# Storing eight blocks of the probability matrix p in six pieces each, without the quarter that is never read back

## The chip, the cores and the metric

The kernel runs on one core of one Trainium2 chip. The metric is the device time of one execution in microseconds (us): the median of 3 runs is 1787.07 us before the change, with runs from 1784.61 to 1787.16. One profiled execution, which took 1786.83 us, gives the trace that is read below.

## What is computed

x is a 2048 x 512 matrix in fp32. Its rows are normalised (xn), and two branches are combined:

```
s   = attention(xn @ wq, k_cache[last 512], v_cache[last 512]) @ wo      32 heads of 128
z   = gelu(x @ w_in);  z1, z2 = first half, layernorm(second half)
g   = silu(((w_sp @ z2 + b_sp) * z1) @ w_out)
out = x + s * g
```

For each head, `scores = q k^T / sqrt(128)`, `p = softmax(scores)` over 512 keys, and `o = p v`. The change lies in the attention, in the way in which p is turned from rows of queries to columns of queries.

## The kernel before

Every fp32 product is made of three matmuls on pairs (high part, low part), written `hi, lo`. The attention works on 128 blocks (`NBLK`): a block b is one head and 512 queries, and has 4 steps of 128 queries, so the loop over t has 512 steps (`NSTEP`) and some lead and tail. In one step TensorE (PE) makes the scores of step t (`score`, L65 to L67 on `qT`), 2 or 3 products of the query projection of a later group (`q_products`, L457), the product of p and v of an earlier block (`pv`, L522 to L524) and the output projection of a still earlier one (`outp`, L65 to L67 on `oT`).

p is made with queries on the partitions, and `pv` needs keys there. The 128 x 512 array of a step is turned in two moves. First VectorE (DVE) transposes 32 x 32 blocks (`turn(t)`, L495) into `pL[b]`, a tile of 128 partitions x 4 x 512. What then stands in partition group i (32 partitions) and part a has to go to partition group a and part i. That is done through DRAM: after the fourth step of a block one DMA stores the whole tile, 128 rows of 8 KB, into `pD[b]` (name p_dram, L499), and two steps later `turned(b)` loads it back in six pieces (L507), in which groups and parts have changed places. The quarter with a = i stays where it is and isn't loaded. From the loaded tile ScalarE casts `pT_h` (`shares`, L514), GpSimd makes `pT_l` (L59), and PE multiplies.

All DMAs named here are issued by SyncE (SP), one after the other in program order, so an issue that waits holds back all that follow it. In each block SP issues the store, loads of weights (`raw`, L105, and in every fourth block two of `wq`, L418), and the six loads of `turned`.

The 64 blocks 0 to 63 work on the first 1024 queries, 64 to 127 on the rest. Near the end of the first half the projection has to change to the other half of x: 28 parts of 256 KB (7 operands `ORDER[k]` with 4 parts n each) are fetched from DRAM by `fetch_part` (L273, names x<-x_dram) at steps 228 + (35 + 34k + 8n)/10, that is in steps 231 to 254, one part per step or a little faster; the matmuls at L457 read them from step 244 on. These steps are those of blocks 57 to 63. The blocks 56 to 63 are the ones that the change touches. Part 28 (k = 6, n = 3) comes in step 254, after the six loads of block 62, and is first read in step 259.

```
for k in range(7):
    for n in range(4):
        ends.setdefault(16 * (NG // 2 - 1) - LEAD + (35 + 34 * k + 8 * n) // 10, []).append((fetch_part, 1, ORDER[k], n))
```

Of the kernel before, what the change touches and what calls it, by code (L numbers as in the profile page):

```python
# [28 lines left out]
NBLK = H * NQ  # L29
# [7 lines left out]
Q = 32  # L37
# [3 lines left out]
def mixer_kernel(ctx: ExitStack, tc: tile.TileContext, x, wh, w_in, w_sp, b_sp, w_out, out):  # L41
# [8 lines left out]
    nc = tc.nc  # L50
# [324 lines left out]
    qps, qT, pps, pD, pL, pT, oT, prob, sums = {}, {}, {}, {}, {}, {}, {}, {}, {}  # L375
# [112 lines left out]
    def turn(t):  # L488

        b, j = divmod(t, 4)
        if j == 0:
            pL[b] = ap.tile([P, 4, 512], F32, name="pL", bufs=4)
        nc.vector.transpose(pL[b][:, :, j * P:j * P + P].rearrange("p a (c q) -> p a c q", q=Q),  # L495
                            prob.pop(t).rearrange("p (a c q) -> p a c q", a=4, q=Q))
        if j == 3:
            pD[b] = dram.tile([4, Q, 4, 512], F32, name="p_dram", bufs=3)
            nc.sync.dma_start(pD[b].rearrange("i r a f -> (i r) (a f)"), pL[b].rearrange("p a f -> p (a f)"))  # L499
            nc.vector.reciprocal(sums[b], sums[b])  # L500

    def turned(b):
# [203 lines left out]
    for t in range(T0, T1):  # L706
# [6 lines left out]
        i = t + XL  # L713
# [33 lines left out]
        if 0 <= t - 1 < NSTEP:  # L747
            turn(t - 1)
# [183 lines left out]
    for r in range(RP):  # L932
        f = WHEN[r, "P6"]
# [88 lines left out]
    for r in range(RP):  # L1022
# [3 lines left out]
        f = WHEN[r, "P6"]  # L1026
# [146 lines left out]
```

## Time and profile before

| | |
|---|---|
| median of 3 runs | 1787.07 us |
| profiled execution | 1786.83 us, its span 1785.0 us |
| PE busy | 1767.4 us, 99% of the span |
| DVE, ACT, POOL busy | 1484.7, 1185.8, 1256.3 us |
| DMA | 402.12 MB, 74.3% of the 16 DMA engines' span on SP's queue |
| p stores (L499) | 128 of 1024 KB, median 4.7 us from issue to landing |
| p loads (L507) | 256 each of 192, 128 and 64 KB, median 4.1, 4.0 and 3.9 us |

The profile's busy times are sums over the whole span. Where an engine had to wait, the trace names what released it. For DMAs it has the time of the issue on SP (SPq) and the time from issue to landing; the share of the DMA engines' time can come out a little over 1 in a short stretch, since packets are counted with their whole duration.

### The profile page before, as it was taken

The numbers are of one execution on the slowest core, as the hardware profiler recorded it, in microseconds if no ns is written. First come the engines' busy times: TensorE is split into PE (matmuls) and PEld (weight loads), VectorE is DVE, ScalarE is ACT, GpSimd is POOL, SyncE is SP. The second block draws the span as 40 slices with busy tenths as digits, with TensorE's granted clock in tenths as the row PEclk, the third lists the DMA queues.
The fourth block names the chain that finished last, engine by engine and source line by source line (L and its number), as shares of the span: only waits on it lengthen the run. The fifth ranks groups of instructions, "written<-read, shape, count | busy, mean of one in ns | idle before, by whom it ended". The sixth has DMA issues, their size and how long they took to land.

```text
span 1785.0 us, 28580 instructions
## 1 busy us (share of the span) xinstructions
PE 1767.4 (99%) x8463; PEld 1513.0 (85%) x8463; DVE 1484.7 (83%) x2451; ACT 1185.8 (66%) x2637; POOL 1256.3 (70%) x1195
## 2 busy tenths in 40 slices
PE   9999999999999999899999999999999999999999
PEld 8788888888888888688888888888888999999997
DVE  6789989899999988788888888888889546887775
ACT  5777777777777776577777777777777546543333
POOL 2788898898888988678888888888888425000033
PEclk9999999999999999999999999999999999999999
DMA  5688887988888989787777787777788652655486
GB/s 202 201 234 246 259 258 224 263 245 240 261 242 247 263 234 291 244 261 228 226 223 224 223 229 217 230 216 231 222 227 256 212 184 87 200 185 171 146 246 210
DMA packets 181180, 402.12 MB, mean 225 GB/s; under 512 B 24096, under 2 KB 61216, under 8 KB 161824
## 3 DMA queue, kind: packets, MB, share of 16 engines
q1 hardware_dynamic: 176416, 394.66, 74.3%
q10 hardware_dynamic: 4608, 5.64, 0.9%
q8 instruction: 66, 1.08, 0.3%
q14 instruction: 90, 0.74, 0.2%
HBM read 233.74 MB, written 166.46 MB: 224 GB/s over the span
## 4 chain that ended last, share of the span: by engine, by line
PE 89%; DVE 4%; DMA 3%; ACT 2%; POOL 1%; issue 1%; SPq 0%; ACTq 0%; DVEq 0%; POOLq 0%
PE ps_a L457 15%; PE ps L67 12%; PE ps L65 12%; PE ps L66 12%; PE ps L881 11%; PE ps_a L524 6%; PE ps_a L522 6%; PE ps_a L523 6%; PE ps_a L65 2%; PE ps_a L66 2%; PE ps_a L67 2%; DMA p_dram<-pL 1%; DMA x<-x_dram 1%; PE ps_f L66 1%; PE ps_f L65 1%; PE ps_f L67 1%
## 5 line engine op out<-in xcount | busy, mean ns | idle before, releaser
L59 POOL TENSOR_TENSOR pT_l<-pL,pT_h 128x512 fp32r<-128x512 f32 x507 | 656.6, 1298 | 189.3 <-ACT pT_h L514 180.4
L486 ACT ACTIVATE prob<-ps,nm 128x512 f32<-128x512 f32 x512 | 354.0, 691 | 337.6 <-DVE nm L484 329.7
L546 DVE SCALAR_TENSOR_TENSOR sacc<-ps,sums,sacc 128x512 f32<-128x512 f32 x496 | 369.9, 746 | 128.5 <-PE ps L67 123.1
L457 PE MATMUL ps_a<-x,x 128*128 128x512 f32 x1302 | 376.7, 390 | 5.7 <-DMA x<-x_dram 5.7
L495 DVE STREAM_TRANSPOSE pL<-prob 128x512 f32<-128x512 f32 x512 | 358.9, 701 | 2.8 <-ACT prob L486 2.8
L484 DVE TENSOR_REDUCE nm<-ps 128x1 f32<-128x512 f32 x512 | 340.4, 665 | 4.9 <-PE ps L67 4.9
L514 ACT CAST pT_h<-pL 128x512 fp32r<-128x512 f32 x512 | 318.5, 622 | 21.8 <-DMA pL<-p_dram 8.5
L457 PEld LDWEIGHTS ps_a<-x,x 128*128 128x128 f32 x1302 | 244.4, 188 | 57.6 <-DMA x<-x_dram 4.7
L59 POOL TENSOR_TENSOR wl<-raw,wh 128x512 fp32r<-128x512 f32 x186 | 241.3, 1297 | 11.3 <-ACT wh L144 11.3
L881 PE MATMUL ps<-b,x 128*128 128x344 f32 x1344 | 212.9, 320 | 3.1 <-POOL b L59 1.3
L881 PEld LDWEIGHTS ps<-b,x 128*128 128x128 f32 x1344 | 212.0, 188 | 3.9 <-POOL b L59 1.5
L524 PE MATMUL ps_a<-pT_l,wh 128*128 128x512 f32 x512 | 200.4, 391 | 1.7 <-POOL pT_l L59 1.5
L65 PE MATMUL ps<-wh,qT_h 128*128 128x512 f32 x512 | 200.0, 391 | 0.8 <-DVE sacc L546 0.8
L522 PE MATMUL ps_a<-pT_h,wh 128*128 128x512 f32 x512 | 200.2, 391 | 0.0
L67 PE MATMUL ps<-wh,qT_l 128*128 128x512 f32 x512 | 199.9, 390 | 0.3
L65 PE MATMUL ps<-wh,oT_h 128*128 128x512 f32 x512 | 199.8, 390 | 0.0
L523 PE MATMUL ps_a<-pT_h,wl 128*128 128x512 f32 x512 | 199.5, 390 | 0.0
L67 PE MATMUL ps<-wh,oT_l 128*128 128x512 f32 x512 | 199.5, 390 | 0.0
L66 PE MATMUL ps<-wl,oT_h 128*128 128x512 f32 x512 | 199.4, 390 | 0.0
L66 PE MATMUL ps<-wl,qT_h 128*128 128x512 f32 x512 | 199.3, 389 | 0.0
L59 POOL TENSOR_TENSOR b<-b 128x688 fp32r<-128x688 f32 (+1 forms) x10 | 18.2, 1820 | 216.6 <-ACT b L1049 188.0
L59 POOL TENSOR_TENSOR x<-wq,x 128x256 fp32r<-128x256 f32 x186 | 138.0, 742 | 1.4 <-ACT x L439 1.4
(206 smaller groups left out, 2998.9 us busy)
## 6 DMA issues: line engine op xcount, KB each, us to landing
p_dram<-pL SPq DMA_DIRECT2D x128, 1024.0 KB, 4.7
pL<-p_dram SPq DMA_DIRECT2D x256, 192.0 KB, 4.1
raw<-wh SPq DMA_DIRECT2D x188, 256.0 KB, 6.2
pL<-p_dram SPq DMA_DIRECT2D x256, 128.0 KB, 4.0
x<-w_sp SPq DMA_DIRECT2D x24, 1024.0 KB, 5.2
pL<-p_dram SPq DMA_DIRECT2D x256, 64.0 KB, 3.9
wq<-wh SPq DMA_DIRECT2D x62, 256.0 KB, 5.8
x_dram<-rawx SPq DMA_DIRECT2D x32, 256.0 KB, 6.1
```

What stands on the lines that cost most here:

```text
L59: engine.tensor_tensor(lo, whole, hi.bitcast(F32), op=OP.subtract)
L65: nc.tensor.matmul(ps, lh, rh, start=first, stop=False)
L66: nc.tensor.matmul(ps, lh, rl, start=False, stop=False)
L67: nc.tensor.matmul(ps, ll, rh, start=False, stop=last)
L457: nc.tensor.matmul(qps[g, bank], wt["q", g, k][a][:, c * P:(c + 1) * P], X[g * 2 // H][ORDER[k]][:, b, c], start=first, stop=r == 5, skip_ ...
L484: nc.vector.tensor_reduce(nm, ps, axis=AX.X, op=OP.max, negate=True)
L486: nc.scalar.activation(prob[t], ps, AF.Exp, bias=nm, accum_out=sums[b][:, j:j + 1])
L495: nc.vector.transpose(pL[b][:, :, j * P:j * P + P].rearrange("p a (c q) -> p a c q", q=Q), prob.pop(t).rearrange("p (a c q) -> p a c q", a ...
L514: nc.scalar.copy(h, p)
L524: nc.tensor.matmul(pps[b], vh, pl, start=False, stop=c == 3)
L546: nc.vector.scalar_tensor_tensor(at, ps, rs, at, op0=OP.mult, op1=OP.add)
L881: nc.tensor.matmul(ps, a, b, start=k != "P4" and c == 0 and m == 0, stop=c == RP - 1 and m == 2, skip_group_check=True)
```

## The change

For the blocks 56 to 63 (b // 8 == 7) the one store of 128 x 2048 is replaced by six stores, of 32 partitions each, which leave out the quarter that `turned` doesn't load. Partition group 0 stores parts 1 to 3, group 1 part 0 and parts 2 to 3, group 2 parts 0 to 1 and part 3, group 3 parts 0 to 2: two of 32 x 6 KB, two of 32 x 4 KB, two of 32 x 2 KB, in all 768 KB. The loads stay as they are.

```
         if j == 3:
             pD[b] = dram.tile([4, Q, 4, 512], F32, name="p_dram", bufs=3)
-            nc.sync.dma_start(pD[b].rearrange("i r a f -> (i r) (a f)"), pL[b].rearrange("p a f -> p (a f)"))
+            if b // 8 == NBLK // 16 - 1:
+                for a in range(4):
+                    for lo, hi in ((0, a), (a + 1, 4)):
+                        if lo < hi:
+                            nc.sync.dma_start(pD[b][a, :, lo:hi], pL[b][Q * a:Q * a + Q, lo:hi])
+            else:
+                nc.sync.dma_start(pD[b].rearrange("i r a f -> (i r) (a f)"), pL[b].rearrange("p a f -> p (a f)"))
             nc.vector.reciprocal(sums[b], sums[b])
```

On SP, the stretch of block 61 before the change, from its store to the first of its loads. DMAHW0 to DMAHW7 are eight landing counters, which SP's DMAs take in turn: a DMA first waits for the landing of the one that had its counter eight DMAs earlier, and the first load also for the store's counter.

```order
L499 DMA p_dram<-pL 128x2048 [waits DMAHW5_49,DVE_49]
L105 DMA raw<-wh 128x512 [waits DMAHW6_49,Pool_49]
L418 DMA wq<-wh 128x512 [waits DMAHW7_49]
L418 DMA wq<-wh 128x512 [waits DMAHW0_49]
L273 DMA x_9049<-x_dram_105 128x512 [waits DMAHW1_49,PE_49]
L273 DMA x_9049<-x_dram_105 128x512 [waits DMAHW2_49]
L507 DMA pL<-p_dram 32x3x512 [waits DMAHW5_49,DMAHW3_49]
```

The same stretch after the change.

```order
L503 DMA p_dram<-pL 32x1536 [waits DMAHW6_49,DVE_49]
L503 DMA p_dram<-pL 32x512 [waits DMAHW7_49]
L503 DMA p_dram<-pL 32x1024 [waits DMAHW0_49]
L503 DMA p_dram<-pL 32x1024 [waits DMAHW1_49]
L503 DMA p_dram<-pL 32x512 [waits DMAHW2_49]
L503 DMA p_dram<-pL 32x1536 [waits DMAHW3_49]
L105 DMA raw<-wh 128x512 [waits DMAHW4_49,Pool_49]
L418 DMA wq<-wh 128x512 [waits DMAHW5_49]
L418 DMA wq<-wh 128x512 [waits DMAHW6_49]
L273 DMA x_9079<-x_dram_105 128x512 [waits DMAHW7_49,PE_49]
L273 DMA x_9079<-x_dram_105 128x512 [waits DMAHW0_49]
L513 DMA pL<-p_dram 32x3x512 [waits DMAHW3_49,DMAHW1_49]
```

What moved: five more DMAs stand ahead of the weights and of two parts of x, and the second wq and the x parts now wait for landings of this block's own first store pieces, where before they waited for loads of the block before. The order of everything else on SP is the same.

The next block, 62, on SP before the change, from its store to its first load.

```order
L499 DMA p_dram<-pL 128x2048 [waits DMAHW4_49,DVE_49]
L273 DMA x_9148<-x_dram_109 128x512 [waits DMAHW5_49]
L105 DMA raw<-wh 128x512 [waits DMAHW6_49,Pool_49]
L273 DMA x_9148<-x_dram_109 128x512 [waits DMAHW7_49]
L507 DMA pL<-p_dram 32x3x512 [waits DMAHW4_49,DMAHW0_49,Pool_49]
```

And after it.

```order
L503 DMA p_dram<-pL 32x1536 [waits DMAHW2_49,DVE_49]
L503 DMA p_dram<-pL 32x512 [waits DMAHW3_49]
L503 DMA p_dram<-pL 32x1024 [waits DMAHW4_49]
L503 DMA p_dram<-pL 32x1024 [waits DMAHW5_49]
L503 DMA p_dram<-pL 32x512 [waits DMAHW6_49]
L503 DMA p_dram<-pL 32x1536 [waits DMAHW7_49]
L273 DMA x_9178<-x_dram_109 128x512 [waits DMAHW0_49]
L105 DMA raw<-wh 128x512 [waits DMAHW1_49,Pool_49]
L273 DMA x_9178<-x_dram_109 128x512 [waits DMAHW2_49]
L513 DMA pL<-p_dram 32x3x512 [waits DMAHW5_49,DMAHW7_49,DMAHW3_49,Pool_49]
```

What moved: the first load of block 62 waits for store pieces where it waited for one store; the six loads and then the last part of x follow it in both programs. No instruction of PE, DVE, ACT or POOL changes its place.

## Rows read from the trace of the kernel before

**Rows 1.** The page: busy time of each engine.

```profile
PE 1767.4 (99%) x8463; PEld 1513.0 (85%) x8463; DVE 1484.7 (83%) x2451; ACT 1185.8 (66%) x2637; POOL 1256.3 (70%) x1195
```

**Rows 2.** Busy time in stretches of 12 us; last: PEclk, DMA share, GB/s.

```profile
648.00:660.00 12.00, 12.00 (x55) 9.93 (x54) 10.45 (x18) 8.49 (x21) 9.52 (x9) 1.00 0.91 246
660.00:672.00 12.00, 12.00 (x55) 9.94 (x54) 10.47 (x18) 10.24 (x25) 10.28 (x10) 1.00 1.01 263
672.00:684.00 12.00, 12.00 (x55) 9.93 (x54) 10.64 (x19) 7.21 (x18) 11.08 (x12) 1.00 0.90 282
684.00:696.00 12.00, 12.00 (x55) 9.93 (x54) 10.76 (x19) 8.70 (x20) 10.57 (x10) 1.00 0.93 292
696.00:708.00 12.00, 12.00 (x55) 9.90 (x54) 10.70 (x18) 7.14 (x17) 6.84 (x7) 1.00 0.90 302
708.00:720.00 12.00, 9.75 (x41) 7.12 (x40) 7.12 (x13) 7.59 (x18) 8.93 (x8) 1.00 0.98 263
720.00:732.00 12.00, 9.62 (x36) 7.49 (x35) 7.51 (x14) 6.15 (x14) 8.71 (x9) 0.86 0.92 281
732.00:744.00 12.00, 10.49 (x46) 8.35 (x45) 9.31 (x17) 7.22 (x19) 7.70 (x8) 1.00 0.76 262
```

**Rows 3.** Timeline of PE: start, duration, in brackets the idle time before it.

```profile
717.52 0.47 PE L457 MATMUL ps_a<-x,x 128*128 128x512 f32 x1 [1.77 <-DMA x<-x_dram]
...
722.90 0.80 PE L457 MATMUL ps_a<-x,x 128*128 128x512 f32 x1 [2.38 <-DMA x<-x_dram]
723.50 0.63 PE L522 MATMUL ps_a<-pT_h,wh 128*128 128x512 f32 x1
723.93 0.63 PE L523 MATMUL ps_a<-pT_h,wl 128*128 128x512 f32 x1
...
733.90 0.74 PE L457 MATMUL ps_a<-x,x 128*128 128x512 f32 x2 [1.51 <-DMA x<-x_dram]
```

**Rows 4.** The chain that ended last, 706 to 736 us: start, duration, what.

```profile
719.85 6.94 DMA p_dram<-pL
...
729.58 4.28 DMA x<-x_dram
```

**Rows 5.** Timeline of SP's queue: start, duration, issues.

```profile
726.86 2.67 SPq L507 DMA_DIRECT2D pL<-p_dram  x6
729.58 0.43 SPq L273 DMA_DIRECT2D x<-x_dram  x1
```

**Rows 6.** SP's queue: issues of single DMAs, from three short windows.

```profile
704.40 0.38 SPq L273 DMA_DIRECT2D x<-x_dram  x1
705.20 0.32 SPq L499 DMA_DIRECT2D p_dram<-pL  x1
...
661.68 0.43 SPq L273 DMA_DIRECT2D x<-x_dram  x1
...
666.75 0.30 SPq L507 DMA_DIRECT2D pL<-p_dram  x1
```

**Rows 7.** The same four, in that order: KB, us from issue to landing.

```profile
x<-x_dram SPq DMA_DIRECT2D x1, 256.0 KB, 4.7
...
p_dram<-pL SPq DMA_DIRECT2D x1, 1024.0 KB, 6.4
...
x<-x_dram SPq DMA_DIRECT2D x1, 256.0 KB, 7.4
...
pL<-p_dram SPq DMA_DIRECT2D x1, 192.0 KB, 5.6
```

**Rows 8.** Stretches in which a store, then twice six loads, were served.

```profile
674.40:676.80 2.40, 2.40 (x12) 2.01 (x11) 2.26 (x4) 0.37 (x2) 2.40 (x3) 1.00 1.04 374
669.10:672.40 3.30, 3.30 (x16) 2.71 (x16) 2.75 (x5) 3.06 (x8) 3.16 (x4) 1.00 1.07 251
718.60:722.40 3.80, 1.93 (x9) 1.25 (x7) 2.54 (x4) 0.00 (x0) 0.00 (x0) 1.00 0.98 217
```

**Rows 9.** SP's own waits, 640 to 740 us: waited for, total, times, longest.

```profile
SPq L507 <- DMA p_dram<-pL: 28.1, 9, 5.8
```

## The prediction

> **What bounds the kernel now.** I read the page first: PE is busy 1767.4 us of a span of 1785.0 [rows 1], so over nearly all of the run only PE's own work counts, and a change of DMAs can show only where PE waits for one. Then the busy times by stretches of 12 us, over the steps that the change touches [rows 2]. PE is busy for 12.00 of 12 us up to 708 us, and then for 9.75, 9.62 and 10.49: it loses 36 - 29.86 = 6.1 us between 708 and 744. In the slice from 720 the granted clock is 0.86 of full speed, so that part of it ran at the lower of the two levels, 1.2 GHz: matmuls start 0.43 us apart there [rows 3], where a full slice of 12 us holds 54 or 55 of them, 0.22 each. That is 0.14 x 12 = 1.7 us more. So the stage holds 7.8 us, or 0.44% of the run, that could be had at most.
>
> The timeline of PE names the cause: three waits of 1.77, 2.38 and 1.51 us, each ended by a landing of x<-x_dram, a part of the other half of x [rows 3]. In the same slices the DMA engines' share is 0.90 to 1.01 [rows 2]. The bound of this stage is the DMA engines. The chain shows how the last wait comes about [rows 4]: the store of block 62 is issued at 719.85 and lands 6.94 us later; only then can SP issue the six loads of block 62 (726.86, 2.67 us for six [rows 5]), and behind them the last part of x, at 729.58, which lands 4.28 us later, at 733.86. PE goes on at 733.90. After it nothing of this kind follows, and PE can't win back what it has lost, as it has no free time elsewhere. So **the effect on the end is the shift of this one landing**, and the sum below counts only what lies ahead of it in the queue. It also follows that the slow stretch of the clock, which lies before the third wait, costs nothing here and gives nothing back: without it PE would only arrive earlier at that wait.
>
> **The change, part by part.** Seven of the eight changed stores (blocks 56 to 62) lie ahead of that landing; block 63's lies behind it.
>
> *Removed: a store of 1024 KB.* What it takes of a busy queue is the distance between its landing and that of the transfer before it. The part of x issued at 704.40 lands 4.7 us later, at 709.1; the store issued next, at 705.20, lands 6.4 later, at 711.6 [rows 6, 7]. So a store costs the queue 2.5 us.
>
> *Added: six pieces, together 768 KB.* No row shows a store from 32 partitions. The lower bound is by bytes at the whole store's rate: 0.75 x 2.5 = 1.9 us. The upper one comes from the six loads, which are of the same sizes and go to 32 partitions each: the part of x issued at 661.68 lands at 669.1, the last of the six loads behind it, issued at 666.75, at 672.4 [rows 6, 7]: 3.3 us for the same 768 KB. In this stretch the engines moved 251 GB/s at a full share, in another one 217, and 374 while a store was served [rows 8]. At 217 GB/s, 768 KB (786,000 bytes) take 3.6 us, and that is the far end. I take 3.3: the loads are the nearest row, in shape and number, and their slowness isn't explained by too few issues, as the share was 1.07. What speaks for the lower end is that the pieces are stores, with runs of 2 to 6 KB where the loads have 2 KB. So each changed block costs the queue 3.3 - 2.5 = 0.8 us more, though it moves a quarter less; seven blocks 5.6 us.
>
> The Trainium skill has a rule on this, in "SBUF — State Buffer", section "Door 1: The DMA port swizzle": a transfer's rate depends on how many of 16 ports its partitions reach, and 32 partitions reach 8 of them. By its asymptote of about 218 GB/s the pieces would take 3.6 us, an estimate from that page, and the sum would end at 1792.5 as in the second rival. The loads of one block agree with the page, those of the other are 15% faster; no run here shows a store.
>
> *What of it is covered.* From 648 to 720 us the shares fall short of 1 by 0.09, 0, 0.10, 0.07, 0.10 and 0.02 [rows 2], together 0.38 x 12 = 4.6 us in which the DMA engines had room. Most of that room lies where SP waits for a store's landing with nothing else to issue (28.1 us in nine waits [rows 9]); there a later landing of the pieces moves the loads too, so I let less than half of the room, 2.0 us, swallow some of the 5.6. If this cover is gone, the whole 5.6 arrives.
>
> *Five more issues per block on SP.* Six issues in a row take 2.67 us [rows 5], so 0.45 each and 2.2 us per block. The weights, two parts of x and the loads stand behind them. I cost this at nothing: the loads wait for the landing of the pieces anyway, and SP's nine waits for that landing are 3.1 us long on average [rows 9]. If that cover is gone, the last block's 2.2 us arrive in full.
>
> *Counters.* With eight landing counters in turn, six pieces use most of them, and the x parts wait for the landing of the same block's first pieces. In a busy queue those land before the pieces behind them, so this is part of the price above. Nothing else moves: the quarter that is left out is never loaded, and no other engine's order changes.
>
> **Sum.** 5.6 - 2.0 = +3.6 us against the profiled execution's 1786.83: 1790.4. That execution stood 0.24 us below the median of 1787.07, so this is 3.3 us or 0.19% over the median. A measurement of this kernel can tell about 0.2% from no change, which is 3.6 us: under 1783.5 is faster, over 1790.6 slower. The forecast lies just inside the upper edge; its own range, with the cover between nothing and 3.5, is 1789 to 1792.5.
>
> **Rivals.**
> *The pieces run at the whole store's rate.* Then each block saves 2.5 - 1.9 = 0.6 us of the queue, seven 4.2: 1782.6, or 1784.0 if starting six pieces costs 0.2 of the 0.6 (0.4 saved a block, 2.8 in all). For it: a store is served at 374 GB/s, and the stage is short of just this. Against it: all that is seen of 32-partition transfers. It decides at 2.5 us for six pieces (2.8 with the cover). Chance 0.20, half of it under 1783.5.
> *The slower row of loads holds.* Six pieces take 3.6 us, +1.1 a block, 7.7 for seven, less 2.0: 1792.5. For it: that stretch was the one nearest to the critical landing. Chance 0.12.
> *Nothing reaches PE.* Pieces at 2.7 to 3.0 us, or a cover of 4.6: within 1.5 us of 1786.8. For it: a share of 0.90 is not full. Chance 0.12.
> *SP becomes the bound.* The issues and counters hold the last part of x back by 2.2 us on top of the forecast: 1792.6. Against it: SP waits in any case. Chance 0.06.
>
> **How the numbers follow.** The forecast has 0.50, nearly half of its range over 1790.6. Slower: 0.24 + 0.12 + 0.06 = 0.42. Faster: half of the first rival, 0.10, and 0.01 for what isn't named. No change: the rest, 0.47. Cases of both signs share the chance, but those with a later landing hold most of it. For 8 in 10 the range goes from 1783.8, which leaves out the better half of the first rival, to 1793.6, which holds the slower loads and SP with 1 us to spare.
>
> **What would show it.** In the profile after, from 646 to 740 us: the distance in landing from the DMA before the first piece to the last piece, in a busy queue; 3.3 us means right, about 2 the first rival. The bytes must fall by 2 MB (8 x 256 KB) and the stores from 128 to 120, with 48 pieces. The landing of the last x part should come about 3.6 us later than 733.9; PE's three waits should grow together, with a first wait of `pT_l` or x before 715. If the DMA share falls below 0.9 and the waits stay, SP was the bound. The forecast is wrong if the three waits shrink, or if PE's lost time moves to another stage.

## The result and the profile after

The changed kernel takes 1790.54 us (median of 22 runs, 1782.44 to 1795.14), the kernel before 1786.47 (22 runs, 1783.21 to 1789.24). The ratio is 1.0023, 95% interval 1.0017 to 1.0030: 4.1 us slower. The forecast was 1790.4.

SP's queue moved 392.57 MB in place of 394.66, and 120 whole stores are left of 128, as the diff says. The time is as forecast. Whether the reasons were, the profile after has to say. Its kernel.py lines behind L499 are those of the kernel before plus 6 (the pieces are L503, the loads L513, pv is L528 to L530); the lines ahead of it are the same. The profiled execution took 1788.65 us, its span is 1786.8.

First the busy times by stretches of 12 us, which answer to [rows 2]. The columns are PE, PEld, DVE, ACT, POOL, then the granted clock, the DMA share and GB/s.

```profile
684.00:696.00 12.00, 11.63 (x52) 9.36 (x51) 9.80 (x18) 8.69 (x20) 10.11 (x9) 1.00 0.96 269
696.00:708.00 12.00, 12.00 (x55) 9.94 (x54) 10.77 (x19) 7.42 (x18) 7.27 (x8) 1.00 0.98 292
708.00:720.00 12.00, 8.75 (x33) 6.29 (x32) 6.51 (x11) 7.29 (x18) 8.91 (x8) 0.91 0.91 229
720.00:732.00 12.00, 10.69 (x43) 8.06 (x41) 9.54 (x17) 6.85 (x16) 8.77 (x9) 0.95 0.87 255
732.00:744.00 12.00, 9.92 (x37) 8.04 (x38) 6.13 (x12) 5.38 (x13) 6.74 (x7) 0.86 0.61 203
```

PE waits for 0.37 + 3.25 + 1.31 + 2.08 = 7.0 us, where it waited 6.1 before. The half-speed clock costs (0.09 + 0.05 + 0.14) x 12 = 3.4 us, where it cost 1.7. Together 10.4 against 7.8: the two traces differ by 2.6 us in this stage, and by 1.8 in their spans. So in these two executions most of the loss is the clock's, and the smaller part is longer waits. This pair of executions holds only part of the loss: the medians differ by 4.1 us. The timeline of PE shows where (start, duration, idle time before in brackets); it answers to [rows 3].

```profile
718.18 0.77 PE L457 MATMUL ps_a<-x,x 128*128 128x512 f32 x1 [2.89 <-DMA x<-x_dram]
718.74 0.63 PE L528 MATMUL ps_a<-pT_h,wh 128*128 128x512 f32 x1
...
720.88 0.60 PE L67 MATMUL ps<-wh,oT_l 128*128 128x512 f32 x1
721.30 0.41 PE L65 MATMUL ps<-wh,qT_h 128*128 128x512 f32 x1
...
722.89 0.51 PE L457 MATMUL ps_a<-x,x 128*128 128x512 f32 x1 [0.26 <-DMA x<-x_dram]
...
734.08 0.73 PE L457 MATMUL ps_a<-x,x 128*128 128x512 f32 x2 [3.13 <-DMA x<-x_dram]
...
735.24 0.63 PE L530 MATMUL ps_a<-pT_l,wh 128*128 128x512 f32 x1
735.66 0.63 PE L65 MATMUL ps<-wh,oT_h 128*128 128x512 f32 x1
...
738.22 0.71 PE L457 MATMUL ps_a<-x,x 128*128 128x512 f32 x2
738.76 0.39 PE L528 MATMUL ps_a<-pT_h,wh 128*128 128x512 f32 x1
```

Matmuls of 0.63 us that start 0.43 apart ran at 1.2 GHz. There are now two such stretches, each behind a wait: up to 721.3, behind the wait of 2.89 us, and from 735.0 to 738.4, behind the last wait of 3.13. The second comes after the last landing that PE waits for, so nothing absorbs it. From that landing PE goes on at 734.08, in the kernel before at 733.90 [rows 3]: 0.18 us and the 1.7 of the second stretch make 1.9, about the difference of the two spans (1.8). Where the other executions lose the rest of the 4.1 us, no trace shows.

Next the price of the six pieces, in the same way as [rows 6, 7]: SP's issues of the part of x ahead of block 61's pieces, of the last of the six, and of the weights behind them, from short windows.

```profile
703.58 0.34 SPq L273 DMA_DIRECT2D x<-x_dram  x1
...
707.47 0.30 SPq L503 DMA_DIRECT2D p_dram<-pL  x1
...
707.92 0.35 SPq L105 DMA_DIRECT2D raw<-wh  x1
```

And from the view of DMAs the same three: KB, us from issue to landing.

```profile
x<-x_dram SPq DMA_DIRECT2D x1, 256.0 KB, 4.9
...
p_dram<-pL SPq DMA_DIRECT2D x1, 192.0 KB, 3.0
...
raw<-wh SPq DMA_DIRECT2D x1, 256.0 KB, 5.6
```

The part of x lands at 708.5 and the last piece at 710.4 or 710.5: **1.9 to 2.0 us** for 768 KB (in blocks 58 and 59 too, 2.4 to 3.0 in 60 and 62). The prediction took 3.3, by the loads; its lower end, by bytes at the whole store's rate, was 1.9. The pieces are cheap where the queue is full. But the weights behind them land at 713.5, 3.0 us after the last piece, where in the kernel before they landed 0.6 us after the store (712.2 against 711.6 [rows 6, 7]). They were issued at 707.92, before at 705.61, because SP had six pieces to issue and the sixth, at 707.47, had to wait for a landing counter. So the queue ran short of work; the two us behind the pieces, in the columns of the first table:

```profile
710.50:712.50 2.00, 2.00 (x10) 1.35 (x8) 1.11 (x4) 1.52 (x4) 2.00 (x3) 1.00 0.78 158
```

The share is 0.78 and the rate 158 GB/s, where the slice from 708 to 720 had 0.91 and 229.

SP's own waits from 648 to 733 us show this for the stage (what it waited for: total, times, longest). The kernel before:

```profile
SPq L507 <- DMA p_dram<-pL: 18.6, 7, 3.6
SPq L507 <- DMA wq<-wh: 3.7, 4, 1.6
SPq L273 <- DMA x<-x_dram: 3.6, 4, 1.2
```

The changed kernel:

```profile
SPq L273 <- DMA x<-x_dram: 6.4, 8, 1.4
SPq L513 <- DMA p_dram<-pL: 4.4, 7, 1.3
SPq L513 <- DMA wq<-wh: 3.5, 4, 1.8
SPq L503 <- DMA pL<-p_dram: 3.3, 8, 0.9
```

The wait for the stores' landing, SP's free time, falls from 18.6 to 4.4 us. The waits for all other landings, which are waits for a counter, rise from 11.0 to 19.1 (the sums of that view's rows; a part of x needs no landing of another part). What was called a cover in the prediction ([rows 9]: 28.1 us in nine waits) is used up.

### The profile page after: what moved, and what is told of

Same layout as the page of the kernel before. It is cut to its first block, busy times and chain, and to the rows that moved or that the text cites. A ratio compares the mean times of both kernels' runs of the same rounds, so it can differ in the third digit from the quotient of the medians.

```text
span 1786.8 us, 28620 instructions
## 1 busy us (share of the span) xinstructions
PE 1768.2 (99%) x8463; PEld 1514.1 (85%) x8463; DVE 1484.5 (83%) x2451; ACT 1185.6 (66%) x2637; POOL 1256.5 (70%) x1195
## 3 DMA queue, kind: packets, MB, share of 16 engines
q1 hardware_dynamic: 177568, 392.57, 74.3%
## 4 chain that ended last, share of the span: by engine, by line
PE 88%; DMA 4%; DVE 3%; ACT 2%; POOL 1%; issue 1%; SPq 1%; ACTq 0%; DVEq 0%; POOLq 0%
PE ps_a L457 15%; PE ps L67 12%; PE ps L65 12%; PE ps L66 12%; PE ps L887 11%; PE ps_a L530 6%; PE ps_a L528 6%; PE ps_a L529 6%; PE ps_a L66 2%; PE ps_a L67 2%; PE ps_a L65 2%; DMA pL<-p_dram 2%; DMA p_dram<-pL 1%; PE ps_f L67 1%; PE ps_f L65 1%
## 5 line engine op out<-in xcount | busy, mean ns | idle before, releaser
L530 PE MATMUL ps_a<-pT_l,wh 128*128 128x512 f32 x512 | 200.9, 392 | 1.6 <-POOL pT_l L59 1.5
L528 PE MATMUL ps_a<-pT_h,wh 128*128 128x512 f32 x512 | 200.4, 391 | 0.0
```

Of the source, the lines that this page charges most:

```text
L530: nc.tensor.matmul(pps[b], vh, pl, start=False, stop=c == 3)
```

## Experiments

Two theories. *Q*, the prediction's: the pieces take more of the queue's time; issues and counters are free. *SP*: the pieces are cheap, and 35 more issues, each with one of eight landing counters, hold back what stands behind them. Changes in us are worked out from the ratio to runs of the kernel before that were taken beside it, times 1786. Intervals are of 95%.

| kernel | extra issues per block | KB per store | ratio | us |
|---|---|---|---|---|
| changed kernel | 5 | 768 | 1.0023 (1.0017 to 1.0030) | +4.1 |
| five issues alone | 5 | 1024 | 1.0047 (1.0035 to 1.0060) | +8.4 |
| three quarters, one store | 0 | 768 | 0.9978 (0.9969 to 0.9986) | -3.9 |
| three pieces | 2 | 896 | 1.0008 (0.9999 to 1.0016) | +1.4 |
| five issues ahead of the loads | 5 | 1024 | 1.0053 (1.0040 to 1.0066) | +9.5 |

### Issues alone

```diff
             nc.sync.dma_start(pD[b].rearrange("i r a f -> (i r) (a f)"), pL[b].rearrange("p a f -> p (a f)"))
+            if b // 8 == NBLK // 16 - 1:
+                for k in range(5):
+                    nc.sync.dma_start(dram.tile([4, P], F32, name=f"tiny{b}_{k}"), ident[32 * (k % 4):32 * (k % 4) + 4, :])
```

> The whole store of 1024 KB as in the kernel before, and behind it in blocks 56 to 63 five DMAs of 2 KB each from a constant tile to places in DRAM that nothing reads. So SP has the changed kernel's six issues and six landing counters a block, with none of its pieces and none of its saving in bytes. Theory Q (the prediction's: the pieces cost the queue more, issues and counters cost nothing): within 1 us of before, ratio 0.9995 to 1.0005. Theory SP (the pieces are cheap, 1.9 us against 2.5 for the whole store, and the loss comes from issues and counters that hold back the weights and parts of x behind them): slower by the 4.1 us of the change and by up to the 4.2 us that its bytes save, so 4 to 8 us, ratio 1.002 to 1.0045, with the first raw part of block 61's step issued about 2 us later than 705.6.

1.0047: 8.4 us slower, a little over the 4 to 8 expected. Theory Q falls; issues with their counters are the whole loss and more. The row from 648 to 733 us of this kernel, and under it that of the kernel before:

```profile
648.00:733.00 85.00, 77.59 (x326) 61.33 (x325) 64.78 (x109) 53.37 (x126) 61.26 (x58) 0.98 0.88 255
```

```profile
648.00:733.00 85.00, 79.76 (x341) 64.25 (x339) 68.65 (x115) 56.23 (x132) 66.27 (x62) 0.98 0.94 276
```

The DMA share falls from 0.94 to 0.88 and the rate from 276 to 255 GB/s: the queue isn't fed. By SP's timeline the first weights of block 61's step go out late:

```profile
709.99 0.32 SPq L499 DMA_DIRECT2D p_dram<-pL  x1
710.36 2.84 SPq L502 DMA_DIRECT2D tiny<-ident  x5
713.34 0.36 SPq L105 DMA_DIRECT2D raw<-wh  x1
713.91 2.86 SPq L418 DMA_DIRECT2D wq<-wh  x2
```

They are issued 3.35 us behind the store, in the kernel before 0.41 (705.20 [rows 6] and 705.61). Landing counters hold SP up as well. Parts of x and `wq` need nothing from the store, yet in this run they wait 9.4 us for its landing (SP's waits, 648 to 733 us), since the DMA eight ahead of them is the store; the kernel before has no such wait:

```profile
SPq L273 <- DMA p_dram<-pL: 6.6, 4, 2.5
SPq L418 <- DMA p_dram<-pL: 2.8, 2, 2.2
```

A part of the 8.4 us is the clock's. Three slices of this run have a granted clock under 1:

```profile
684.00:696.00 12.00, 10.25 (x37) 7.46 (x37) 6.90 (x13) 6.80 (x16) 7.17 (x8) 0.86 0.81 259
732.00:744.00 12.00, 7.18 (x25) 5.29 (x24) 5.24 (x9) 5.17 (x12) 7.96 (x8) 0.78 0.83 218
744.00:756.00 12.00, 12.00 (x51) 9.89 (x50) 9.43 (x16) 6.75 (x16) 6.72 (x7) 0.94 0.62 201
```

That is (0.14 + 0.22 + 0.06) x 12 = 5.0 us at half speed, where the kernel before has 1.7. So 8.4 us is what these issues cost this kernel, its clock included, and not what an issue costs by itself.

### Bytes alone

```diff
-            nc.sync.dma_start(pD[b].rearrange("i r a f -> (i r) (a f)"), pL[b].rearrange("p a f -> p (a f)"))
+            if b // 8 == NBLK // 16 - 1:
+                nc.sync.dma_start(pD[b].rearrange("i r a f -> (i r) a f")[:, :3], pL[b][:, :3])
...
-                    nc.sync.dma_start(pL[b][Q * a:Q * a + Q, lo:hi], of[a, :, lo:hi])
+                    nc.sync.dma_start(pL[b][Q * a:Q * a + Q, lo:hi], of[a % 3 if b // 8 == NBLK // 16 - 1 else a, :, lo:hi])
```

> One store of 768 KB in place of 1024 KB in blocks 56 to 63: every partition's first three quarters, and the last partition group loads the quarter of the group at 2 in place of its own, so the fourth quarter is left out and that group's weights are not the reference's. The bytes of the six pieces with one issue and one counter. Theory SP: the bytes are worth what the landings say, 2.5 - 1.9 = 0.6 us a block, up to 4.2 us: 2 to 4 us faster than before, ratio 0.9977 to 0.999. Theory Q has nothing against that for a store from 128 partitions. A third theory, that the saved bytes fall where the queue has room and reach nothing: within 1 us of before, and then the whole loss of the change is SP's.

0.9978: 3.9 us faster. So the bytes that the change leaves out are worth what the landings say, 0.6 us a block. This kernel leaves out a quarter that is needed; it measures time only. The two parts add up: 8.4 - 3.9 = +4.5, and the change measured +4.1. The intervals of the two are wide (6.3 to 10.7 and 2.5 to 5.5 us), so that so close a sum is partly chance.

### Where, and how many

*Pieces in blocks 61 and 62 alone* (the changed kernel with `if b in (61, 62):`).

> Six pieces in blocks 61 and 62 alone, the whole store in 56 to 60 and 63. Theory SP: what decides is the stretch in which SP issues the pieces of block 61 and the weights behind them, since the queue runs dry there; most of the 4 us of the change is here: 3 to 5 us slower than before. Theory Q: two blocks of seven, 0.8 us each: at most 1.6 us slower. If the loss were gathered over all blocks through the counters: about 1 us slower.

1.0013 (1.0005 to 1.0021), 2.3 us. It lies between the values expected (about 1, at most 1.6, and 3 to 5), and its interval, 0.9 to 3.8 us, reaches into all of them; the run doesn't settle whether the loss gathers over all blocks or arises near the end.

*Three pieces*: the first and the last partition group without their own quarter, the two middle ones whole.

```diff
+                for g, n, lo, hi in ((0, 1, 1, 4), (1, 2, 0, 4), (3, 1, 0, 3)):
+                    nc.sync.dma_start(pD[b].rearrange("i r a f -> (i r) a f")[Q * g:Q * (g + n), lo:hi], pL[b][Q * g:Q * (g + n), lo:hi])
```

> The store in three pieces in blocks 56 to 63: the first partition group without its own quarter, the two in the middle whole, the last without its own: 896 KB with two issues more than the whole store, half the saving of the six pieces with two fifths of their extra issues. By the two runs on issues alone (+8.4 us for five, 1.7 for one) and bytes alone (-4.0 us for 256 KB), if both are proportional: 2 x 1.7 - 2.0 = +1.4 us over before, ratio 1.0003 to 1.0013. By the prediction's theory, 32 partitions at the loads' rate for two of the pieces: 2 to 4 us slower. If any extra issue is free as long as few are added: 2 us faster.

1.0008, +1.4 us, as the two prices said before it ran: 2 x 1.7 for two issues per block, less 2.0 for an eighth of the bytes. Its interval, -0.2 to 2.9 us, excludes the 2 us faster; it holds both no change and the lower end of what the prediction's theory gave (2 to 4).

*The five issues at another place*, in `turned`, ahead of the six loads.

> The five small DMAs of the first run, now not behind the store but ahead of the six loads, where SP waits for the store's landing in the kernel before (18.6 us in seven waits). The weights and parts of x that stand behind the store are then no longer behind the five issues. If what costs is that these are issued 2.2 us later: within 2 us of before, ratio 0.999 to 1.001. If what costs is the number of landing counters taken (eight in turn, and each DMA waits for the one eight ahead of it) or SP's whole time: 5 to 9 us slower, as with the five behind the store.

1.0053, +9.5 us: as dear as behind the store. So it isn't that the weights stand behind the issues; they cost the same at both places, by their counters or by SP's whole time.

*The pieces on ScalarE's queue* (`nc.scalar.dma_start` for the pieces).

> The changed kernel with its six pieces issued from the ScalarE queue instead of SP's; SP then has no store to issue in blocks 56 to 63 and the raw weights and parts of x are not queued behind them. Theory SP: the loss goes and the saving in bytes shows: 1 to 4 us faster than before, that is 5 to 8 us under the changed kernel, unless ScalarE is held up by the wait for the transposes (six issues of 0.45 us, 2.7 us a block, against a ScalarE that is busy 66% of the span). Theory Q: as the changed kernel, about 4 us slower than before, since the same pieces take the same time of the DMA engines.

1.0088 (1.0074 to 1.0102), 15.7 us slower: a miss. The timeline of ACT shows why:

```profile
657.64 5.09 ACTq L503 DMA_DIRECT2D p_dram<-pL  x6
662.77 0.62 ACT L520 CAST pT_h<-pL 128x512 fp32r<-128x512 f32 x1 [5.84 <-DMA p_dram<-pL]
```

Six issues that take 2.7 us without waits took 5.09, so they waited 2.4 us among themselves; ScalarE did nothing else for 5.84 us, and pT and the softmax behind them were late. The queue was another, but the landing counters seem to be shared: SP's parts of x, `wq` and raw weights, which need nothing from these stores, waited 13.8 us for their landing (648 to 733 us).

### The last landing

The prediction said that the effect on the end is the shift of the last part of x. One edit, to each kernel, has it issued a step earlier, ahead of block 62's loads:

```diff
-            ends.setdefault(16 * (NG // 2 - 1) - LEAD + (35 + 34 * k + 8 * n) // 10, []).append((fetch_part, 1, ORDER[k], n))
+            ends.setdefault(16 * (NG // 2 - 1) - LEAD + min((35 + 34 * k + 8 * n) // 10, 25), []).append((fetch_part, 1, ORDER[k], n))
```

In the kernel before:

> The kernel before with the same edit: whole stores, and the last part of x one step earlier, ahead of block 62's six loads. It lands at about 729.7 in place of 733.86 and PE reaches it at 732.39: the third wait of 1.51 us is gone. If the last landing sets the end: 1.5 us faster than before, ratio 0.9988 to 0.9996, and the best correct kernel so far. If PE then waits for the weights of block 62, whose loads come 0.4 us later: within 0.7 us of before.

0.9986 (0.9977 to 0.9995): 2.5 us faster, and the fastest version of this study with the whole computation. Its stretches:

```profile
708.00:720.00 12.00, 9.71 (x41) 7.16 (x40) 9.02 (x15) 7.74 (x20) 8.96 (x8) 1.00 1.03 273
720.00:732.00 12.00, 10.58 (x45) 8.12 (x46) 7.88 (x14) 6.40 (x17) 9.05 (x9) 1.00 1.01 322
732.00:744.00 12.00, 12.00 (x55) 9.93 (x54) 10.68 (x18) 9.64 (x23) 10.71 (x10) 1.00 0.59 200
```

The wait behind 732 is gone, and so is the half-speed stretch; PE loses 2.29 + 1.42 = 3.7 us against 7.8 [rows 2], 4.1 less, as much as its span is shorter (1780.9 against 1785.0). Not all of that is the edit's. SP issued the three parts of x ahead of block 62's store, which the edit doesn't move, 3.1 us earlier in this execution; the kernel before and then this run:

```profile
717.40 2.35 SPq L273 DMA_DIRECT2D x<-x_dram  x3
```

```profile
714.29 2.58 SPq L273 DMA_DIRECT2D x<-x_dram  x3
```

The 2.5 us between the runs are the measure of the edit, and that the half-speed stretch is gone by it isn't shown. In the changed kernel:

> The changed kernel with one edit: the last part of x is fetched one step earlier, so SP issues it ahead of block 62's six loads and not behind them. The prediction held that the effect on the end is the shift of this one landing. In the changed kernel it lands at 734.04, and PE, which reaches it at 730.95, then waits 3.13 us and runs 3.4 us at half speed, which costs another 1.7. Ahead of the loads it would land at about 731.1, one part of x (0.7 us) behind the one at 730.41. So by the prediction's theory of the landing, with the clock's stretch behind it: 3 to 4.7 us under the changed kernel, ratio to before 0.9995 to 1.0007. If the loss sits in the first waits and is only passed on: 1 us or less under the changed kernel.

1.0018 (1.0010 to 1.0027): about 0.9 us under the changed kernel, not told apart from it, at the "passed on" end. So with x early the six pieces cost 5.7 us (1.0018 against 0.9986), no less than the 4.1 without. The timeline of PE has no wait behind 727, but

```profile
720.69 0.47 PE L457 MATMUL ps_a<-x,x 128*128 128x512 f32 x1 [1.35 <-DMA x<-x_dram]
...
726.61 0.50 PE L457 MATMUL ps_a<-x,x 128*128 128x512 f32 x1 [2.96 <-DMA x<-x_dram]
```

that last wait is followed by half speed again (0.86 from 720 to 732), and PE has waited 1.2 us before 696 and 2.6 from 708 to 720. In the kernel before, the last landing moves the end. In the changed kernel the parts of x before it are late as well.

### Fewer issues

x in 14 DMAs of 512 KB in place of 28 of 256 KB takes 14 issues away. The pairs go out in the step of their first part, so the measure for them is a kernel with 28 parts at the same steps:

```diff
-            ends.setdefault(16 * (NG // 2 - 1) - LEAD + (35 + 34 * k + 8 * n) // 10, []).append((fetch_part, 1, ORDER[k], n))
+            ends.setdefault(16 * (NG // 2 - 1) - LEAD + (35 + 34 * k + 16 * (n // 2)) // 10, []).append((fetch_part, 1, ORDER[k], n))
```

> The kernel before, with every second part of x issued in the step of the part ahead of it, still 28 DMAs of 256 KB. It is the measure for the two runs with pairs, which issue at the same steps. The last part goes ahead of block 62's loads as in the run with the whole store and x early (-2.1 to -2.5 us); others go ahead of a store of 1024 KB that they stood behind, or ahead of six loads. If the order of the queue alone decides: 2 to 5 us faster than before, ratio 0.997 to 0.999. If SP then waits longer for x's buffers, nothing beyond 2 us.

0.9991 (0.9982 to 1.0000): 1.6 us faster, less than expected. Then the pairs:

```diff
-        nc.sync.dma_start(X[w][k][:, n % 2, n // 2].bitcast(F32), xd[w, k][:, n % 2, n // 2])
+        nc.sync.dma_start(X[w][k][:, :, n // 2].bitcast(F32), xd[w, k][:, :, n // 2])
...
-        for n in range(4):
+        for n in range(0, 4, 2):
```

> Whole stores, and x in 14 DMAs of 512 KB in place of 28 of 256 KB: 14 issues and 14 counters fewer, same bytes, same steps as the run with parts a step early. By the price of an issue with its counter, 8.4 us / 35 = 0.24: 3.4 us under that run. If issues cost only where they are more than SP has room for (in the kernel before it waits 18.6 us for landings of stores): within 1 us of that run. If the coarser landing costs (the first product of a pair waits for 512 KB in place of 256): up to 3 us over it.

0.9997 (0.9988 to 1.0005), no gain over the parts, though SP now stands idle for twice as long:

```profile
SPq L507 <- DMA p_dram<-pL: 37.7, 8, 7.1
```

PE's one long wait there is for a pair of x:

```profile
719.09 0.77 PE L457 MATMUL ps_a<-x,x 128*128 128x512 f32 x1 [4.28 <-DMA x<-x_dram]
```

So with whole stores fewer issues are worth nothing; or they are worth something and the coarser landing takes it back. The third run has the same pairs, with the six pieces.

> The changed kernel's six pieces with x in 14 DMAs of 512 KB: 35 issues more and 14 fewer than the kernel before. If each issue has one price wherever it stands: 4.1 us over the run with whole stores and pairs, as the change is over before. If issues cost only above what SP has room for, 21 more than before cost less and the saving of 4.0 us in bytes shows: between 2 us over and 4 us under the run with whole stores and pairs. The prediction's theory, that the pieces take the queue's time: 4 us over it, and the landing distance of six pieces 3.3 us; the profile of the changed kernel says 1.9.

0.9995 (0.9986 to 1.0004), and 0.9997 with whole stores: between these two kernels the six pieces cost nothing that shows, where they cost 4.1 us with x in 28 DMAs. It isn't the last part's earlier place that does it, since the pieces cost 5.7 us with x early. Either the change's loss depends on how many DMAs stand around it, or PE's long wait for a pair (4.28 us with whole stores, 3.12 with pieces) sets the time of both kernels and hides the pieces; no run separates these. The intervals leave room for about 2 us between the two, so the 3.9 us in bytes don't come through in full, and how much of them does is open. Last, three pieces with pairs, all in all the issues of the kernel before:

> The store in three pieces (896 KB, 16 issues more in blocks 56 to 63) and x in 14 DMAs of 512 KB (14 fewer): all in all the kernel before's number of issues and counters, 1 MB less in bytes, and the last part of x ahead of block 62's loads. With the issues even, half the 4.0 us of the run on bytes alone should be left, and the 1.6 us of the run with parts a step early: 2 to 3.6 us faster than before, ratio 0.998 to 0.999, at or under the run with whole stores and x early (0.9986). If the coarse landing of the pairs binds, as one wait of 4.28 us in the run with whole stores and pairs suggests: within 1.5 us of that run, ratio 0.999 to 1.0003.

0.9990 (0.9981 to 0.9999), 1.8 us faster; SP's wait for the stores is back at the kernel before's size (20.5 us, 18.6 there):

```profile
SPq L511 <- DMA p_dram<-pL: 20.5, 12, 3.8
```

It is a little under the expected range, and within 1.5 us of the run with whole stores and pairs, which was expected if the coarse landing binds. It is not told apart from the whole stores with x early (0.9986). Both beat the kernel before, by 1.8 and 2.5 us; the simpler edit is as good.

## Why the number was right and the reasons were not

The forecast's +3.6 us (to 1790.4) was met by +4.1 (1790.54). Its sum was 5.6 of queue time less 2.0 of cover. What the runs show is a saving of 3.9 and a cost of 8.4: **two errors of opposite sign**. The pieces were put 9.5 us too high (+5.6 for -3.9), the issues 8.4 too low, and 2.0 were taken off for a cover of which no run shows anything. That the sum came out is luck.

*What bounds the kernel*: right. The DMAs of this stage do, as the run on bytes shows (a quarter less of eight stores, 3.9 us faster). One reading was off: the share of 0.90 to 1.01 holds up to 732 us, and the slice with the third wait has 0.76 [rows 2].

*"Removed: a store of 1024 KB", 2.5 us*: consistent with the run on bytes, 0.6 us a block for a quarter of it.

*"Added: six pieces, I take 3.3"*: failed. It is 1.9 to 2.0 in a busy queue, the lower bound. Shape and number of the loads were the wrong likeness: 768 KB in six stores took three quarters of the whole store's time. The sentence on the Trainium skill, "SBUF — State Buffer", "Door 1: The DMA port swizzle", falls with it: by the 218 GB/s of 32 partitions the six would take 3.6 us, and 786,000 bytes in 1.9 are 414 GB/s. That figure is for 32 partitions, which reach 8 ports. Here pieces of all four groups stand in the queue together, and they are stores; which of the two makes the difference wasn't tested, and a piece by itself was not measured.

*"Five more issues per block on SP. I cost this at nothing"*: failed, and it is the main error. 35 issues with their counters cost 8.4 us, 0.24 each in this kernel. The cover named for it was SP's wait for the stores' landing, 28.1 us in nine waits [rows 9]. Two of these, together 9.4 us, are for the loads of blocks 55 and 63 and lie outside the stage (640 to 648 and 733 to 740 us); 18.6 us in seven waits are left. An issue takes 0.45 us [rows 5], so 35 of them take 15.6, and they took nearly all of that wait: 18.6 us became 4.4. The waits were long in sum, but SP was idle there only because it had run ahead; without that lead the weights and parts of x go out when the queue has already run short.

*"Counters ... part of the price"*: failed with it. A piece of 64 KB takes one of eight counters as a store of 1024 KB does. So what can be under way at once shrinks in bytes: block 61's weights landed 3.0 us behind the pieces, with the engines at a share of 0.78.

*"The effect on the end is the shift of this one landing"*: right for the kernel before (taking that landing out of the way gave 2.5 us), not shown for the changed one (0.9 of 4.1, within the noise). The landing itself came at 734.04, where it had been at 733.86 [rows 4], with a trace that ran up to 0.9 us earlier ahead of the stage; not 3.6 later.

*"The slow stretch of the clock ... costs nothing here and gives nothing back"*: this may hold for the place it speaks of, ahead of the third wait. What it missed is that the change can make a second stretch: behind the longer last wait there is one, and it costs 1.7 us, nearly all of the profiled execution's loss.

*The rivals.* "The pieces run at the whole store's rate" had the price right (1.9) and the time wrong, for the same free issues. "SP becomes the bound" had the place right, at a chance of 0.06, and asked for the pieces to be dear as well. The test that the prediction set, "3.3 us means right, about 2 the first rival", came out at 2; the other one, a DMA share below 0.9, holds for 720 to 744 us (0.87, 0.61, [rows 2]: 0.92, 0.76) and not clearly ahead of it. PE's three waits, which were to grow together, went from 1.77, 2.38 and 1.51 us [rows 3] to 2.89, 0.26 and 3.13.

What stays open: how the cost divides between SP's 0.45 us per issue and the landing counter. Both go together in every run. That counters hold DMAs back is seen in the 9.4 us that x and `wq` wait for the store's landing in the run with five issues, and in ScalarE's six issues, which took 5.09 us in place of 2.7; how much of the end it makes, no run shows, since none took one away and left the other. A time that each small DMA takes from the DMA engines isn't separated either; that their share fell to 0.88 in the run with five issues speaks against it.

## What to carry to other kernels

Splitting a DMA to save bytes costs issues and landing counters, and those have a price of their own even where the queue that issues them looks idle: count the issues per period against the time that the queue has, and ask whether that time is its lead. Measure the two parts apart (issues with no bytes, bytes with no issues); they added up here to within 0.4 us, with intervals that leave room for more, and neither could be read from the other. The price belongs to the kernel around it: with x in pairs the six pieces cost nothing that shows. A forecast that comes out can still rest on two errors that cancel: compare its own tests in the profile, here the landing distance, before trusting it.

## What the runs showed of the hardware that was not expected

Six stores from 32 partitions each took 1.9 to 2.0 us for 768 KB, three quarters of one store from 128 partitions, where six loads to 32 partitions each took 3.3.

A DMA of 2 KB isn't free: five of them per block cost 1.2 us a block in this kernel, though they carry no bytes to speak of.

The DMA share says little of room: over 648 to 733 us it is 0.94 in the changed kernel as before, with 253 GB/s in place of 276.

```profile
648.00:733.00 85.00, 79.07 (x337) 63.47 (x335) 68.79 (x115) 55.19 (x130) 65.35 (x62) 0.98 0.94 253
```

PE's half-speed stretches came behind waits for x: of 2.38 us (before), 2.89 and 3.13 (changed), and 2.96 (changed with x early), among others. The execution with whole stores and x early had none. Each of these stretches costs 1.7 us of work at half speed; how much of that reaches the end depends on whether a wait lies behind it.
